# A scheduled RWKV and Fourier-mixing kernel: the first token DFT split in three, idle TensorE multiplications early, and a new order of all operations

## The chip, the cores and the metric

The kernel runs on one core of one Trainium2 chip. The metric is device time in microseconds (us), the median of the executions that are not disturbed. The kernel before took 244.32 and 245.5 us in its two undisturbed runs; a third, of 280.6 us, was slow (over 1.5% above the fastest of the same kernel), which is left out of comparisons.

TensorE (PE in the profile; its weight loads are PEld) multiplies, VectorE (DVE), ScalarE (ACT) and GpSimd (POOL) do the rest, SyncE (SP) issues most transfers (184 of 189 in the profile of before). One undisturbed execution of the same kernel differs from another by up to 1.4 per cent here, so differences of 1 us need many runs, and single profiles are compared only stretch by stretch.

## The reference

Four batches, eight heads, 768 tokens, head size 40. A recurrence over tokens, then a Fourier mixing with a small two-layer network on the 320 columns of all heads:

```python
for t in range(S):
    y[:, :, t] = einsum('bhd,bhde->bhe', r[t], state)
    Sa = einsum('bhde,bhe->bhd', state, a[t])
    state = state * w[t][:, :, None, :] - einsum('bhd,bhe->bhde', Sa, b[t]) \
            + einsum('bhd,bhe->bhde', v[t], k[t])
x = y.transpose(0, 2, 1, 3).reshape(B, S, 320)
u = x + real(fft(fft(x, axis=1), axis=2))        # token DFT, then column DFT
un = (u - mean(u)) / sqrt(var(u) + 1e-6)
out = u + relu(un @ w_ch1) @ w_ch2
```

## The kernel before

The kernel cuts the 768 tokens of a batch into six chunks of 128. Within a chunk the recurrence becomes matrix products. One function describes every operation once, with the engines that may run it; nothing is issued yet:

```python
# logarithm of the decay, split into a bf16 high part and a rest ("low")
op({"ACT": ... nc.scalar.activation(lg(), n_["w"](), Act.Ln)}, w=[logw], kind="ln")
op({"POOL": ..., "DVE": ... tensor_tensor(low, lg, hi, Alu.subtract)}, w=[low], r=[logw], kind="low")
# cumulated decays on TensorE, exponentials rw and wp on ScalarE, and the inputs scaled with them:
for j, nm, s_ in ((0, "k", rw), (2, "a", wp), (1, "b", rw)):
    op(scaled(nt[j], n_[nm], s_), kind="scale")               # VectorE or GpSimd, tile "nat"
# turned on TensorE, copied out of PSUM (kb, ar, vt), multiplied with each other,
op({"DVE": ... tensor_tensor(d_(), p2(), mask, Alu.mult),     # 128 x 1024 out of PSUM
    "ACT": ... activation(d_(), p2(), Act.Copy)}, kind="evac")
...
# the state
op({"DVE": ... tensor_tensor(s32(), Q(), wt(), Alu.mult)}, w=[s32], r=[Q, wt], kind="s32")
op({"ACT": ..., "DVE": ..., "POOL": ...copy(s16T, s32)}, w=[s16T], r=[s32], kind="s16T")
...
# tables of sines for the DFT: 15 small VectorE operations (tiles it, h), then ScalarE
# token DFT of a batch over its folded chunks (pm), in parts given by SPLIT
SPLIT = ((), (), (), (5,))
for c0, c1 in splits:
    for T in range(3): ... zmm(T, c0, c1)                     # kind "z"
```

Which engine runs what, in which order, and in which buffer, is written down in two strings, made by a search outside the kernel. `run` walks along them:

```python
def run(self, order, slots, warm):
    for i, e in order:
        if e == "WARM":
            warm(i // 64, i % 64)      # an idle multiplication into a free PSUM bank
            continue
        o = self.ops[i]
        before = set(o.preds) | self.take(o, slots)
        o.alts[e][1]()                 # issue it on engine e
        ...
```

Each engine works through its own operations strictly in that order: in the traces of before every engine's operations start in the order written (407 on VectorE, 3642 multiplications on TensorE).

## Time and profile before

| before | value |
|---|---|
| span of the profiled execution | 242.8 us |
| busy: TensorE, VectorE, ScalarE, GpSimd | 92%, 87%, 75%, 64% |
| VectorE's first eviction of a product (reading it out of PSUM, tile pr) | 16.52 us |
| VectorE's first addition of mixed values (hand-over) | 68.45 us |
| VectorE up to the hand-over: at work, idle | 61.81, 6.64 us |
| TensorE time lost after the hand-over | 13.5 us |

"Lost" is the distance between the starts of neighbouring TensorE instructions beyond their pace when dense, as the prediction defines it. Where TensorE is dense at full clock in the traces of before, the median distance is 25 ns for 40 columns, 56 for 128, 136 for 320 and 162 for 384, and of 64 rows and 128 columns two start every 55 to 56 ns. Turned means transposed.

### The profile page before, as it was taken

How to read it: one execution, taken by the hardware profiler on the slowest of the kernel's cores; microseconds unless marked ns; L12 is line 12 of the kernel's file. 1: busy time of each engine (PE TensorE's matmuls, PEld its weight loads, DVE VectorE, ACT ScalarE, POOL GpSimd, SP SyncE). 2: the span in 40 equal slices, each digit the busy share in tenths (PEclk: the TensorE clock that was granted, in tenths of full speed). 3: DMA queues.
4: the chain of work that ended last, by engine and by line, in shares of the span. 5: the costliest groups of instructions: out<-in, count | busy, mean ns of one | idle time of the engine just before them, and what ended most of it. 6: DMA issues, size and time to landing. Idle time of an engine off the chain costs nothing.

```text
span 242.8 us, 8954 instructions
## 1 busy us (share of the span) xinstructions
PE 223.3 (92%) x3642; PEld 172.9 (71%) x3642; DVE 210.2 (87%) x407; ACT 182.0 (75%) x379; POOL 156.5 (64%) x247
## 2 busy tenths in 40 slices
PE   0668979899999998999999999999999999999994
PEld 0436857778887776778887777788887778876672
DVE  6997999999899999979899998999999988488432
ACT  3595989898999987872799965974899988164620
POOL 7372594988896857845886878858996774510000
PEclk9995899999999999999999999999999999999999
DMA  7999999999773999999989999999899940011103
GB/s 121 187 184 157 189 163 159 160 158 162 122 128 52 180 170 133 166 162 185 162 160 244 182 166 178 162 167 150 214 175 165 146 47 4 3 54 63 47 27 135
DMA packets 171833, 33.94 MB, mean 140 GB/s; under 512 B 167120, under 2 KB 171472, under 8 KB 171792
## 3 DMA queue, kind: packets, MB, share of 16 engines
q1 hardware_dynamic: 170112, 31.73, 75.6%
q0 software_dynamic: 1680, 1.64, 4.8%
q8 instruction: 28, 0.46, 0.8%
q14 instruction: 13, 0.11, 0.1%
HBM read 26.87 MB, written 3.93 MB: 127 GB/s over the span
## 4 chain that ended last, share of the span: by engine, by line
PE 63%; DVE 18%; ACT 7%; issue 4%; SPq 3%; DMA 1%; POOL 1%; DVEq 0%; POOLq 0%
PE ps L152 63%; DVE h L152 4%; DVE pr L152 3%; DVE m L152 2%; SPq L416 2%; DMA in<-in_v_dram 1%; ACT pr L152 1%; DVE s L152 1%; SPq L752 1%; DVE xb L152 1%; DVE ps L152 1%; DVE ar L152 1%; DVE nat L152 1%; DVE xs L152 1%; ACT un L152 1%
## 5 line engine op out<-in xcount | busy, mean ns | idle before, releaser
L152 PE MATMUL ps<-unT,w1sb 128*128 128x384 bf16 x240 | 47.4, 326 | 0.4 <-ACT m L152 0.3
L454 POOL TENSOR_TENSOR nat<-in,rw 128x320 bf16<-128x320 f32 x41 | 35.7, 877 | 9.6 <-ACT rw L152 4.0
L152 DVE TENSOR_TENSOR pr<-ps,su 128x1024 bf16<-128x1024 f32 x31 | 37.4, 1216 | 1.4 <-PE ps L152 0.6
L152 PEld LDWEIGHTS <-nat 128*128 128x128 bf16 x512 | 31.4, 101 | 8.6 <-DVE nat L152 3.5
L152 ACT ACTIVATE pr<-ps 128x1024 bf16<-128x1024 f32 x33 | 33.4, 1028 | 3.8 <-PE ps L152 3.7
L152 PE MATMUL ps<-w2sb,h 128*128 128x320 bf16 x240 | 35.2, 299 | 0.0
L152 PEld LDWEIGHTS <-pr 128*128 128x128 bf16 x768 | 29.2, 96 | 6.8 <-issue 0.9
L152 PE MATMUL ps<-ident,nat 128*128 128x128 bf16 x352 | 31.6, 228 | 2.5 <-DVE nat L152 2.5
L447 POOL TENSOR_SCALAR_AFFINE_SELECT pr<-pr 128x1024 bf16<-128x1024 bf16 x28 | 30.6, 1096 | 4.9 <-ACT pr L152 4.7
L152 ACT ACTIVATE h<-ps 128x384 bf16<-128x384 f32 x56 | 26.5, 498 | 5.9 <-PE ps L152 5.6
L152 PEld LDWEIGHTS <-h 128*128 128x128 bf16 x240 | 22.7, 98 | 8.6
L152 PEld LDWEIGHTS <-w1sb 128*128 128x128 bf16 x240 | 20.6, 97 | 10.9 <-issue 0.6
L647 POOL TENSOR_TENSOR pm<-xb 128x161 bf16<-128x161 f32 x42 | 21.6, 530 | 7.0 <-DVE xb L152 6.9
L467 POOL TENSOR_TENSOR low<-logw 128x320 f16<-128x320 f32 x22 | 16.1, 736 | 13.8 <-issue 6.5
L454 POOL TENSOR_TENSOR nat<-in,wp 128x320 bf16<-128x320 f32 x20 | 17.6, 880 | 8.7 <-ACT wp L152 8.5
L152 PE MATMUL ps<-ar,kb 64*128 64x128 bf16 x384 | 18.1, 221 | 2.5 <-DVE kb L152 0.7
L152 DVE TENSOR_TENSOR m<-ps,su 128x1024 bf16<-128x1024 f32 x15 | 18.2, 1218 | 1.5 <-PE ps L152 1.4
L152 DVE SCALAR_TENSOR_TENSOR xb<-ps,bst,xb 128x320 f32<-128x320 f32 x24 | 12.8, 543 | 7.5 <-PE ps L152 5.8
L152 PE MATMUL ps<-nat,pr 128*128 128x40 bf16 x384 | 17.3, 180 | 0.5 <-DVE pr L152 0.4
L152 PE MATMUL ps<-xs,pr 128*128 128x40 bf16 x384 | 17.4, 181 | 0.2
L152 PEld LDWEIGHTS <-kb 64*128 64x128 bf16 x384 | 11.9, 95 | 7.1 <-issue 2.2
L152 ACT ACTIVATE sn<-ps 128x320 bf16<-128x320 f32 x22 | 9.8, 444 | 8.5 <-PE ps L152 7.9
(144 smaller groups left out, 573.8 us busy)
## 6 DMA issues: line engine op xcount, KB each, us to landing
in<-in_w_dram SPq DMA_DIRECT2D x24, 160.0 KB, 4.1
in<-in_v_dram SPq DMA_DIRECT2D x24, 160.0 KB, 3.7
in<-in_r_dram SPq DMA_DIRECT2D x24, 160.0 KB, 3.9
in<-in_a_dram SPq DMA_DIRECT2D x24, 160.0 KB, 3.9
in<-in_k_dram SPq DMA_DIRECT2D x24, 160.0 KB, 4.1
in<-in_b_dram SPq DMA_DIRECT2D x24, 160.0 KB, 3.9
out_dram<-xb SPq DMA_DIRECT2D x24, 160.0 KB, 2.3
w2sb<-in_moe_w_ch_dram POOLq DMA_DIRECT2D x2, 400.0 KB, 8.6
```

The source lines that it names most:

```text
L152: i = f(*args, **kwargs)
L416: op({"SP": (0.7, lambda x_=x_, t_=t_: nc.sync.dma_start(x_(), t_[bb, :, c * C:(c + 1) * C, :].rearrange("h t d -> t h d")))}, w=[x_], dma ...
L447: op({"POOL": (0.035 + 0.563 * n_, lambda d_=d_: nc.gpsimd.affine_select(out=d_(), in_=d_(), compare_op=Alu.is_gt, fill=0.0, base=0, patte ...
L454: return {"POOL": (0.82, lambda: nc.gpsimd.tensor_tensor(dst(), x_(), s_(), Alu.mult)), "DVE": (cD(320), lambda: nc.vector.tensor_tensor(d ...
L467: op({"POOL": (0.68, lambda: nc.gpsimd.tensor_tensor(low()[:, :, :D], lg(), hi()[:, :, :D], Alu.subtract)), "DVE": (cD(320), lambda: nc.ve ...
L647: op({"POOL": (0.46, lambda a_=a_, f_=f_: nc.gpsimd.tensor_tensor(*a_(), f_)), "DVE": (0.33, lambda a_=a_, f_=f_: nc.vector.tensor_tensor( ...
L752: op({"SP": (0.42, lambda c=c: nc.sync.dma_start(out[bb, c * C:(c + 1) * C], xb()[:, c, :DM]))}, r=[xb[c]], dma=0.5, kind="out")
```

## The change

The intent: keep TensorE's clock up early with idle multiplications (that they do so was my assumption), do the first batch's token DFT in parts as its chunks end, take PSUM banks beside held ones, drop a copy of the state, and search a new order under these rules. The diff, cut to its core (the strings are 46 and 11 lines long and change almost wholly; the rest is code for options that are switched off, and costs that only the search uses):

```diff
-ORDER = ("HWDAQDAUDAEDAHDAVDAIDAMGACGAAGAbSADGARDA+SBEAAfSCEGCFGCJDCIDCRDCGDABGAPDCLDBhSCHDAgSAXDASDAhAATGAiD"
...
+ORDER = ("AIDASDAJDAHDACGAFDARDA+SBEAABGCEGADGAbSAUDAQDAhABhSAgSAEDBFDAAGCFGA-WA-WA-WA-WA-WA-WAvWBJPBKAATDCHD"
...
-SPLIT = ((), (), (), (5,))
+SPLIT = ((3,5),(),(),(5,))
...
-            op({"DVE": ... nc.vector.tensor_tensor(s32(), Q(), wt()..., Alu.mult)}, w=[s32], r=[Q, wt], kind="s32")
-            op({... copy(d_(), s32())}, w=[s16T], r=[s32], kind="s16T")
+            if c == NCH - 2:
+                s32 = None
+                op({"DVE": ... nc.vector.tensor_tensor(d_(), Q(), decay(), Alu.mult)}, w=[s16T], r=[Q, wt], kind="s32")
+            else:
+                ... as before
```

A triple in ORDER is an operation and its engine; W stands for an idle multiplication. Which PSUM bank an operation takes is written in SLOTS alone.

## The prediction

> **What bounds the kernel now.** I began with the page's busy shares and its forty slices, to see whether one engine bounds the whole span. Its columns are tenths of busy time, one digit for 6.07 us.
>
> ```profile
> span 242.8 us, 8954 instructions
> PE 223.3 (92%) x3642; PEld 172.9 (71%) x3642; DVE 210.2 (87%) x407; ACT 182.0 (75%) x379; POOL 156.5 (64%) x247
> PE   0668979899999998999999999999999999999994
> DVE  6997999999899999979899998999999988488432
> PEclk9995899999999999999999999999999999999999
> ```
>
> The reader is to see two regimes. In the first eleven slices (67 us) VectorE is nearly always at 9 while TensorE has holes; after that TensorE is solid at 9. Only slices 4 and 5 have a reduced TensorE clock.
>
> TensorE's 92% overstates its load, because overlapping matmuls are counted to their modelled ends. So I summed what its instructions need at the pace of the dense stretches (columns / 2.4 GHz + 2.5 ns, never under 25 ns, half of that for the paired 64-row ones): 197.9 us, the six idle multiplications included. From its first matmul (5.59 us) to its last (239.2) pass 233.6 us, so 35.6 us are lost to waits and slow clock. By stretch: up to 68.4 us 22, from 68.4 to 239.6 us 13.5 (170.6 us for 157.1 us of work, 8%). Before the first matmul lie 5.6 us, after the last one 3.7.
>
> Next I took the stretches around the slow clock, and the chain of waits there.
>
> ```profile
> core 0: us, PE busy (x) PEld busy (x) DVE busy (x) ACT busy (x) POOL busy (x), PEclk, DMA share, GB/s
> 18.00:27.00 9.00, 8.19 (x119) 6.59 (x114) 7.21 (x12) 6.16 (x13) 2.15 (x4) 0.62 1.05 167
> 27.00:68.40 41.40, 38.22 (x816) 32.04 (x815) 38.84 (x59) 38.27 (x81) 35.15 (x53) 1.00 0.95 159
> 68.40:239.60 171.20, 169.03 (x2643) 129.38 (x2639) 147.59 (x302) 126.36 (x267) 107.76 (x151) 1.00 0.75 131
> ```
>
> ```profile
> 17.65 1.22 DVE pr L152
> 18.87 0.05 issue
> 18.91 2.82 PE ps L152 x39
> 21.75 0.70 DVE ar L152
> 22.50 9.26 PE ps L152 x161
> ```
>
> From 18 to 27 us TensorE is on the chain and VectorE has 1.8 us idle. From 27 to 68 us VectorE is busy 38.84 of 41.4 us: that stretch is VectorE's. From 68 us on TensorE alone is full (169.0 of 171.2).
>
> Last I took single instructions, for the clock itself and for the first batch's token DFT (columns: start, duration, engine; in brackets the idle time before it and who ended it):
>
> ```profile
> 19.37 0.43 PE L152 MATMUL ps<-logw,ut 128*128 128x320 bf16 x1
> 19.59 0.47 PE L152 MATMUL ps<-low,ut 128*128 128x320 f16 x1
> 19.85 0.63 PE L152 MATMUL ps<-ident,nat 128*128 128x128 bf16 x4
> ...
> 28.41 0.30 PE L152 MATMUL ps<-logw,ut 128*128 128x320 bf16 x1
> 28.55 0.30 PE L152 MATMUL ps<-low,ut 128*128 128x320 f16 x1
> ...
> 65.97 1.22 DVE L152 TENSOR_TENSOR m<-ps,su 128x1024 bf16<-128x1024 f32 x1 [0.85 <-PE ps L152]
> 68.45 0.49 DVE L152 TENSOR_TENSOR xb<-ps,xb 128x320 f32<-128x320 f32 x1
> ```
>
> The same 320-column matmul is followed after 0.26 us at 19.59 and after 0.14 us at 28.41: half the clock and the full clock. At 65.97 VectorE waits 0.85 us for a product that stands behind the token DFT (three groups of 12 column blocks, about 1 us each) in TensorE's order. The last line is VectorE's first addition of the mixed values (call it the hand-over): from there post-processing of batch 0 overlaps batch 1's chunks.
>
> [...] its clock records change at 12.36, 19.19 and 26.01 us, two gaps of 6.83 us[...]. [...]
>
> **The change, part by part.** I counted the operations of both programs and their order on each engine.
>
> 1. Clock. Idle multiplications go from 6 (2,712 columns) to 28 (11,760), nine of them before the first real matmul and 24 before batch 0's second chunk is far along. They use no other engine. In the slow stretch from 19.2 to 26.0 us TensorE did work worth 3.25 us at full pace in 6.9 us. If the clock holds, at most 3.6 us of that come back. But VectorE had only 1.8 us idle between 18 and 27, and it sets the rest: I count 1.5 us. The slow stretch before 12.4 us costs little, since the chain there runs over VectorE's tables.
>
> 2. VectorE's work before the hand-over. With the mean of each kind from the trace of before, its list up to there sums to 61.1 us before and 59.95 after: fewer wide evictions (24 to 22, 1.15 us each), scalings (6 to 3, 0.49) and zero fills (11 to 9), one select and one fold less, against 8 more small copies of turned tiles (0.43 each) and two more low parts (0.37). That is 1.1 us saved on the engine that bounds this stretch. Against it, fewer fills leave VectorE idle before the first logarithm (finished at 5.17 us): about 2.3 us idle at the start, where before had 1.7. Net 0.5 us.
>
> 3. Token DFT in three parts. The same matmuls, split 3 + 2 + 1 chunks. In the new order all nine groups still stand after the last chunk's output matmuls, within 14 TensorE operations, so they are not moved into early gaps. What is gained is that only 3 groups of 0.17 us wait for the last fold, and other work goes between: the 0.85 us wait at most; I count 0.5. The three banks are held only briefly.
>
> 4. State copy. In the last but one chunk of each batch the decayed state is written in bf16 directly: four copies fewer (0.4 us on ScalarE, 0.87 on VectorE), about 0.4 us off each batch's recurrence, which bounds nothing: 0.
>
> 5. The rest of the order. Counts for TensorE are the same, and at the first mixing matmul both kernels have the same 157.8 us of real TensorE work ahead. The gain of the first regime therefore goes through undiminished, and the second changes only by its 13.5 us of losses. A new order with retuned costs might take a tenth off these, but also lose it: I count 0.6 us of gain, give or take 2.
>
> Sum: 1.5 + 0.5 + 0.5 + 0.6 = 3.1 us. The two undisturbed runs of before, 244.32 and 245.5, average 244.9, so I predict 241.8 us, a ratio of 0.987. The hand-over should move from 68.45 to about 66 us.
>
> **Rivals.** (a) The clock's gain is wholly hidden: VectorE is busy at 9 through the first 67 us, so a faster TensorE only waits more. It speaks for this that slices 3 to 11 are VectorE's, against it that VectorE idled 1.51 us at 23.95 for TensorE. The time would be 243.5 to 245. (b) Idle multiplications get in the way: at half the clock their 10,400 early columns take 8.7 us in place of 4.4, in an in-order queue. A group of five (2,496 columns) stands before the third product of chunk 0; cold it takes 2.1 us. VectorE has three 1.2 us evictions to do meanwhile, so I expect at most 1 us. The time would be 245 to 247. (c) The order pays in the second regime: taking a third of its 13.5 us away would give 238. Nothing in the trace shows a large single wait to remove there (its longest named TensorE waits are under 0.5 us), so I hold it unlikely.
>
> **Range and chances.** Independent errors of about 1 us (clock), 1 us (VectorE's start) and 2 us (losses of the second regime) combine to 2.4 us, which with 8 in 10 gives 3.1: 238.8 to 244.9. Two per cent faster means under 240.0, which is 0.75 of such an error below the centre: 0.22. Two per cent slower means over 249.8: 0.03. Within: 0.75.
>
> **What would show it.** Right: a granted clock of 1.0 from about 12 us on, the 320-column pair near 20 us 0.14 us apart, the hand-over at 65 to 67 us, no 0.85 us wait before it, and 170 to 171 us of TensorE after it. Clock right but nothing gained (a): a hand-over after 67.5 us with VectorE busy throughout. (b) would show as first evictions later than 16.5 us. The prediction is wrong if the stretch after the hand-over changes by more than 3 us, or if the hand-over comes before 64 us, which VectorE's 59.95 us of work hardly allow.

## More of the kernel before

An operation that has to wait holds up everything behind it on its engine: in before, SyncE waits 13.2 us for the input of one transposing transfer, issues it at 75.08 us, and the loads behind it from 77.23 us on.

"At work" counts an operation to its end or to the start of the next; VectorE's very first fill, 0.27 us in every kernel, is counted as idle.

The prediction shows the page and the windows from 18 us on. It has nothing of the first 18 us but the clock, which turned out to be its gap. This is VectorE's timeline there (start, duration, engine, line, operation, output<-input, shapes):

```profile
7.50 0.43 DVE L152 TENSOR_TENSOR low<-logw 128x320 f16<-128x320 f32 x1
...
10.23 0.99 DVE L152 TENSOR_SCALAR h<-h 128x320 f32<-128x320 f32 x1
11.15 2.08 DVE L152 SCALAR_TENSOR_TENSOR h<-h,h 128x320 f32<-128x320 f32 x2
13.15 0.48 DVE L152 TENSOR_TENSOR nat<-in,wp 128x320 bf16<-128x320 f32 x1
...
15.14 1.33 DVE L152 TENSOR_SCALAR nsu<-su 128x128 bf16<-128x128 bf16 x1
15.91 0.68 DVE L152 COPY kb<-ps 128x1024 bf16<-128x1024 bf16 x1
16.52 1.21 DVE L152 TENSOR_TENSOR pr<-ps,su 128x1024 bf16<-128x1024 f32 x1
```

Two things are to be seen. The low part and the scaled input (nat<-in,wp), which TensorE waits for, stand behind small operations on the sine tables (h), which nobody needs before about 60 us. And some of these small operations are far longer than they need: 0.99 us for one on 320 columns, of which others take 0.32 us here, 2.08 us for the next two, and 1.33 us for the negation of a 128x128 mask.

## The result, and the profile after

The changed kernel took 237.97 us (four runs, 237.01 to 239.15); the kernel before, beside it, 244.58 in its three undisturbed runs (245.04 with the slow one). The ratio is 0.972, with an interval of 0.966 to 0.979: faster by 2.8%. A ratio is the mean time of one kernel's fast runs over that of the other's in the same rounds, so not quite the ratio of the medians. I timed the changed kernel twice more: 239.66 against 244.75 (0.980, 0.974 to 0.986) and 237.55 against 243.26 (0.976, 0.971 to 0.980), medians of fast runs. So the gain is 2 to 2.8%, about 5 to 7 us. I had predicted 3.1 us and held 238.8 as the lowest likely time; the prediction was wrong.

The page after (busy time; the forty slices):

```profile
span 235.7 us, 8993 instructions
...
PE 224.1 (95%) x3664; PEld 170.7 (72%) x3664; DVE 208.0 (88%) x411; ACT 182.3 (77%) x378; POOL 153.5 (65%) x242
...
PE   7878999889999999999999999999999999999994
...
DVE  6999999999999998998999999999899998689342
...
PEclk9999999999999999999999999999999999999999
```

TensorE begins in the first slice, with idle multiplications, and its granted clock has no hole from the first clock record (5.79 us) on. Before its first record the page prints full clock, but that isn't what ran: up to then idle multiplications of 504 columns start 0.42 us apart, half the pace of those at 9.05 us and later (0.21 us). The same goes for the kernel before up to 12.36 us (320-column matmuls 0.26 us apart at 8.51 us), whatever the rows for 0 to 18 us below say. The same stretches as in the prediction, with the first 18 us added (columns as there: PE, PEld, DVE, ACT, POOL busy, clock, DMA), first after, then the one line of before that was not shown:

```profile
0.00:18.00 18.00, 14.14 (x151) 7.62 (x152) 15.66 (x38) 12.40 (x26) 9.16 (x38) 1.00 0.97 160
18.00:27.00 9.00, 8.00 (x162) 5.91 (x159) 8.74 (x17) 8.97 (x17) 7.08 (x14) 1.00 1.00 171
27.00:63.40 36.40, 34.33 (x732) 28.60 (x728) 34.73 (x54) 32.58 (x71) 33.71 (x50) 1.00 0.95 161
63.40:232.50 169.10, 167.66 (x2631) 128.59 (x2628) 148.47 (x306) 128.33 (x269) 103.54 (x143) 1.00 0.80 138
```

```profile
0.00:18.00 18.00, 7.86 (x81) 4.86 (x81) 16.04 (x36) 11.21 (x21) 11.49 (x40) 1.00 1.02 164
```

The stretch between 27 us and the hand-over shrank from 41.4 to 36.4 us, the one after it from 171.2 to 169.1. GpSimd works 9.16 us in the first 18 in place of 11.49. From 18 to 27 us VectorE is now full, with 17 operations where it had 12.

The chain of waits after, where before had TensorE for 9.26 us from 22.50 on (start, duration, what; the longest pieces):

```profile
2.69 4.00 DMA in<-in_r_dram
...
10.82 1.01 ACT kb L160
...
13.40 1.22 DVE pr L160
...
17.70 2.32 ACT tk L160 x2
```

Its longest piece up to 26.7 us is now an input transfer, of 4.00 us: the start waits for data where it waited for tables. After that come pieces of ScalarE and VectorE: a copy on ScalarE, the first eviction, the sines. TensorE at half the clock is gone from it.

Clock and hand-over after (rows of TensorE, then of VectorE):

```profile
20.27 0.30 PE L160 MATMUL ps<-logw,ut 128*128 128x320 bf16 x1
20.41 0.30 PE L160 MATMUL ps<-low,ut 128*128 128x320 f16 x1
```

```profile
58.66 1.23 DVE L160 TENSOR_TENSOR m<-ps,su 128x1024 bf16<-128x1024 f32 x1
...
63.36 0.49 DVE L160 TENSOR_TENSOR xb<-ps,xb 128x320 f32<-128x320 f32 x1
```

The pair of 320-column matmuls is 0.14 us apart at 20 us, the last masked product before the hand-over no longer waits, and the hand-over comes at 63.36 us, 5.1 us earlier. Of these 5.1 us, VectorE's work makes 3.25 (61.81 to 58.56) and its idle time 1.84 (6.64 to 4.80). The work repeats in the two other profiles of the changed kernel (58.64 and 58.53), the idle time does not (5.99 and 4.83).

VectorE's start after, to be held against the block above:

```profile
2.85 0.13 DVE L160 TENSOR_SCALAR nsu<-su 128x128 bf16<-128x128 bf16 x1
...
5.64 0.49 DVE L160 TENSOR_TENSOR low<-logw 128x320 f16<-128x320 f32 x1
...
8.27 0.49 DVE L160 TENSOR_TENSOR nat<-in,wp 128x320 bf16<-128x320 f32 x1
...
13.40 1.21 DVE L160 TENSOR_TENSOR pr<-ps,su 128x1024 bf16<-128x1024 f32 x1
```

The mask takes 0.13 us at 2.85 us instead of 1.33 us at 15.14. The low part comes 1.9 us earlier and the scaled input 4.9 us earlier, with 14 and 8 of the 15 table operations still to come; the three copies of turned tiles are gone to ScalarE. The first eviction starts at 13.40 instead of 16.52 us (12.73 and 12.41 in the two other profiles).

The stretched operations of before have GpSimd at work beside them: GpSimd of before runs operations from 10.16 us to beyond 16.5 with at most 0.17 us between them, which is where 0.99, 2.08 and 1.33 us stand; after, it waits 6.82 us for an input, until 12.09. The first of them, in before:

```profile
10.16 0.88 POOL L454 TENSOR_TENSOR nat<-in,rw 128x320 bf16<-128x320 f32 x1 [3.84 <-ACT nat L152]
```

Over all operations of VectorE before the hand-over that took over 0.2 us more than the fast quarter of the same operation and shape, the excess is 3.5 us in the profile of before, and 1.2, 0.9 and 0.7 us in three profiles of the changed kernel. That GpSimd's work is the cause is read from this coincidence; no experiment of mine switched it alone, and how it would act is not shown. All twenty profiles together make the coincidence hard to escape: of 607 VectorE operations that worked on SBUF alone (statistics and fills left out) while GpSimd did nothing, none was stretched by over 0.2 us; of 458 with GpSimd busy for half their time or more, 191 were; of 5,763 that read or wrote PSUM, none was, whatever GpSimd did. So in these profiles GpSimd beside it is needed for a stretch, but is not enough. Counted in this way over all profiles, the stretching before the hand-over is 2.9 to 4.1 us in the seven that begin in the old order, and 0 to 1.5 us in twelve that begin in the new one; after_old_list has 2.6.

### The profile page after: what moved, and what is told of

It reads as the page before. It is cut to its first block, busy times and chain, and to the rows that moved or that the text cites.

```text
span 235.7 us, 8993 instructions
## 1 busy us (share of the span) xinstructions
PE 224.1 (95%) x3664; PEld 170.7 (72%) x3664; DVE 208.0 (88%) x411; ACT 182.3 (77%) x378; POOL 153.5 (65%) x242
## 4 chain that ended last, share of the span: by engine, by line
PE 52%; DVE 16%; ACT 12%; issue 6%; DMA 5%; POOL 4%; SPq 3%; DVEq 0%; POOLq 0%; ACTq 0%
PE ps L160 52%; DVE pr L160 4%; SPq L433 3%; DVE xb L160 2%; POOL nat L472 2%; DMA in<-in_k_dram 2%; DMA in<-in_r_dram 2%; DVE xs L160 1%; DMA in<-in_w_dram 1%; DVE sm L160 1%; ACT kb L160 1%; DVE h L160 1%; ACT L160 1%; ACT tk L160 1%; DVE un L160 1%
## 5 line engine op out<-in xcount | busy, mean ns | idle before, releaser
L160 PE MATMUL ps<-unT,w1sb 128*128 128x384 bf16 x240 | 45.9, 326 | 0.4 <-DVE xb L160 0.4
L465 POOL TENSOR_SCALAR_AFFINE_SELECT pr<-pr 128x1024 bf16<-128x1024 bf16 x31 | 34.4, 1116 | 8.9 <-ACT pr L160 8.7
L160 DVE TENSOR_TENSOR pr<-ps,su 128x1024 bf16<-128x1024 f32 x28 | 33.9, 1217 | 3.0 <-PE ps L160 2.6
L160 PEld LDWEIGHTS <-nat 128*128 128x128 bf16 x512 | 29.8, 97 | 7.6 <-DVE nat L160 1.5
L160 PE MATMUL ps<-ident,nat 128*128 128x128 bf16 x352 | 30.5, 219 | 1.2 <-DVE pr L160 0.3
L685 POOL TENSOR_TENSOR pm<-xb 128x161 bf16<-128x161 f32 x40 | 19.9, 523 | 2.8 <-DVE xb L160 2.8
L472 POOL TENSOR_TENSOR nat<-in,wp 128x320 bf16<-128x320 f32 x18 | 15.9, 881 | 8.5 <-PE ps L160 4.0
L160 DVE TENSOR_SCALAR h<-ps 128x384 bf16<-128x384 f32 x24 | 12.8, 551 | 3.4 <-PE ps L160 1.8
L488 POOL TENSOR_TENSOR low<-logw 128x320 f16<-128x320 f32 x17 | 12.2, 719 | 4.9 <-ACT logw L160 3.3
L160 DVE TENSOR_TENSOR m<-ps,su 128x1024 bf16<-128x1024 f32 x12 | 14.6, 1219 | 0.6 <-PE ps L160 0.5
```

Of the source, the lines that this page charges most:

```text
L160: i = f(*args, **kwargs)
L465: op({"POOL": (0.12 + 0.48 * n_, lambda d_=d_: nc.gpsimd.affine_select(out=d_(), in_=d_(), compare_op=Alu.is_gt, fill=0.0, base=0, pattern ...
L472: return {"POOL": (0.82, lambda: nc.gpsimd.tensor_tensor(dst(), x_(), s_(), Alu.mult)), "DVE": (cD(320), lambda: nc.vector.tensor_tensor(d ...
L488: op({"POOL": (0.68, lambda: nc.gpsimd.tensor_tensor(low()[:, :, :D], lg(), hi()[:, :, :D], Alu.subtract)), "DVE": (cD(320), lambda: nc.ve ...
L685: op({"POOL": (0.48, lambda a_=a_, f_=f_: nc.gpsimd.tensor_tensor(*a_(), f_)), "DVE": (0.33, lambda a_=a_, f_=f_: nc.vector.tensor_tensor( ...
```

## The experiments

Eighteen runs were made, of fifteen other kernels and three repeats; all gave correct results. They are told by the question they were to answer. Edits are written with names of operations in place of the codes of ORDER. "Ahead at W" is how much earlier than in the kernel before TensorE has done W us of useful work (idle multiplications not counted, each instruction at its dense pace). A caution first: with almost the same start, before_idle, before_direct_state and before_early_low have their hand-over at 67.39, 67.39 and 67.19 us, against 68.45 in the profile of before. About 1 us of its lateness is therefore the luck of that one execution, and of the 5.1 us a fairer figure is 4. The two other profiles of the changed kernel have theirs at 64.63 and 63.36, so single hand-overs differ by 1.3 us with nothing changed. Times and ranges in the table are over all runs; ratios use fast runs alone. Five rows hold slow runs: the medians of their fast runs are 237.71 (after_no_idle), 240.75 (after_no_idle_again), 239.46 (after_one_dft), 238.53 (after_late_low, two runs left) and 242.73 (before_direct_state).

| kernel | time (range, runs) us | ratio to before (95%) | hand-over us | VectorE work + idle up to it us |
|---|---|---|---|---|
| after_again | 239.66 (238.56–241.92, 6) | 0.980 (0.974–0.986) | 64.63 | 58.64 + 5.99 |
| after_third | 237.55 (236.75–238.83, 6) | 0.976 (0.971–0.980) | 63.36 | 58.53 + 4.83 |
| after_no_idle | 239.07 (237.03–241.78, 4) | 0.979 (0.972–0.987) | 63.22 | 58.88 + 4.35 |
| after_no_idle_again | 241.30 (239.03–243.99, 17) | 0.985 (0.981–0.988) | 63.08 | 58.38 + 4.70 |
| after_one_dft | 239.56 (237.89–244.1, 6) | 0.978 (0.972–0.985) | 64.81 | 58.42 + 6.39 |
| after_late_low | 241.14 (237.95–243.22, 4) | 0.975 (0.966–0.984) | 64.02 | 58.99 + 5.03 |
| after_old_list | 240.46 (239.36–242.35, 4) | 0.987 (0.981–0.993) | 65.95 | 61.22 + 4.73 |
| after_old_rest | 242.63 (241.56–243.83, 15) | 0.996 (0.994–0.999) | 63.74 | 57.80 + 5.94 |
| before_idle | 243.82 (242.63–245.39, 20) | 1.001 (0.999–1.003) | 67.39 | 61.79 + 5.60 |
| before_early_low | 243.68 (243.0–246.04, 20) | 1.000 (0.998–1.002) | 67.19 | 61.25 + 5.94 |
| before_direct_state | 242.75 (241.64–246.02, 20) | 0.996 (0.993–0.998) | 67.39 | 60.99 + 6.39 |
| before_all_parts | 246.66 (245.47–247.34, 6) | 1.013 (1.008–1.017) | 70.33 | 59.79 + 10.55 |
| before_front_new_rest | 246.43 (245.48–247.33, 4) | 1.012 (1.007–1.016) | 69.05 | 60.98 + 8.07 |

The kernels not in the table are told below with their times.

### Is it the clock?

after_no_idle and after_no_idle_again are the same kernel, the changed one without idle multiplications:

```diff
 ORDER of the changed kernel
-28 x W (idle multiplication)
```

> The kernel after with all 28 idle multiplications taken out, nothing else. Theory 1 (the clock carries the first stretch): [...] the hand-over (VectorE's first addition of mixed values, 63.36 us after, 68.45 before) comes at 66.5 us or later and the time rises by 3.5 us or more over the kernel after, to 241.5 us or more. Theory 2 (the new order of the first 20 us carries it, by relieving VectorE): the time rises by less than 1.5 us, to under 239.5 us. My prediction's own figure for the clock, 1.5 us, would give 239.5 us.

> The changed kernel without its 28 idle multiplications, timed more closely. Theory clock (the early full clock carries what my prediction gave it, 1.5 us or more): 1.5 us or more above after_again. Theory start-up list (what VectorE does first decides; the idle multiplications only steady the clock): within 1.0 us of after_again, with the wider spread from run to run.

> The changed kernel as it is, for a closer comparison with the two runs beside it. All theories: median between 237.0 and 239.2 us, ratio to the kernel before 0.970 to 0.980.

before_idle puts 18 idle multiplications early into the kernel before:

```diff
 ORDER of the kernel before
+8 x W before the first matmul, 10 x W between the first chunk's turns, products and its X
```

> The kernel before with 18 more idle multiplications of 504 columns in TensorE's early gaps (8 before the first real matmul, 10 between 12 and 19 us), order otherwise untouched. Theory 1 (clock): the clock is full from about 9 us on, the hand-over comes at 65.5 us or earlier, and the time falls by 3 us or more, to 242 us or less. Theory 2 (front order): VectorE's tables and fills still fill the first 16.5 us, so the time falls by 2 us at most, to 243 to 244.5 us, all of it from the stretch 18 to 27 us.

Without idle multiplications the clock was low until 9.40 us and again from 16.2 to 19.6 (in the repeat until 12.65 and from 16.1 to 19.5), and yet the hand-over came at 63.22 and 63.08 us, no later than with them. So no part of the early hand-over that these profiles can resolve is the clock's doing. With them in the kernel before, the clock was full from 11.8 us on, the hand-over 1.06 us earlier, as in other kernels without them, and the time the same (1.001). Where the whole time is concerned, the changed kernel was slower without them by 1.1 us in the medians of the fast runs of the same rounds and by 0.0044 in the ratios, which is 1.1 us of 245; the intervals overlap. So they may be worth about 1 us, not shown firmly, and not by way of the hand-over. I don't know the way.

The profile of after_no_idle_again shows what else can move single runs. It reached the hand-over first of all and then lost about 4 us against after_no_idle, between 63 and 80 us. These are the rows of GpSimd and VectorE there, then the same VectorE operation in after_no_idle with the GpSimd operation beside it:

```profile
74.74 0.44 POOL L531 CAST nat<-in 128x320 bf16<-128x320 f32 x1
75.15 0.85 POOL L471 TENSOR_TENSOR nat<-in,rw 128x320 bf16<-128x320 f32 x1
75.97 1.08 POOL L464 TENSOR_SCALAR_AFFINE_SELECT pr<-pr 128x1024 bf16<-128x1024 bf16 x1
```

```profile
75.62 3.18 DVE L159 TENSOR_SCALAR un<-xb,bst 128x320 bf16<-128x320 f32 x1
```

```profile
73.07 0.86 POOL L471 TENSOR_TENSOR nat<-in,rw 128x320 bf16<-128x320 f32 x1
73.65 0.47 DVE L159 TENSOR_SCALAR un<-xb,bst 128x320 bf16<-128x320 f32 x1
```

The same instruction took 0.47 us in one execution and 3.18 us in the other, in which GpSimd worked without a gap from 74.74 to about 79 us. In the first GpSimd was as busy (from 69.1 to 77.1 us), so a busy GpSimd alone doesn't decide; what does, these runs don't show. Before that, GpSimd had waited 2.17 us for an input transfer at 64.7 us, which it had not in the other. A late transfer shifts GpSimd against VectorE; that this shift made the collision is my reading of the two profiles, not shown by a run.

### Is it the DFT in three parts?

```diff
-SPLIT = ((3,5),(),(),(5,))
+SPLIT = ((),(),(),(5,))
 ORDER of the changed kernel
-z(chunks 0-2) x3, z(chunks 3-4) x3
```

> The changed kernel with the first batch's token DFT in one part again, its three groups of multiplications where the last part stood; all else as it is. Theory split (the prediction's third part, 0.5 us): 0.3 to 0.8 us above after_again. Rival: within 0.3 us, since in the order of the change all nine groups stand within 14 TensorE instructions of each other behind the last chunk, so that nothing is taken out of the hand-over by splitting.

It took 239.46 us in its fast runs, the changed kernel on the same chip 239.66. That fits the rival: the split is worth nothing that these runs resolve. But each ratio is known to about 0.006, or 1.5 us, so a gain of 0.5 us would not have been seen either. All nine groups stand within 14 TensorE instructions of each other behind the last chunk, with the split too.

### Is it VectorE's start?

after_late_low undoes one thing, before_early_low does some things alone:

```diff
 VectorE in the changed kernel (after_late_low)
-tab, low(chunk 0), 6 x tab, low(chunk 2)
+7 x tab, low(chunk 0), low(chunk 2)
```

```diff
 VectorE in the kernel before (before_early_low)
-fill(w1sb), zero fills, 6 x tab, low(chunk 0), 9 x tab, ... mask nsu between the copies
+zero fills, mask nsu, 3 x tab, low(chunk 0), 12 x tab, ... fill(w1sb) after the evictions
 SyncE
-load w(chunk 0), load w(chunk 1)
+load w(chunk 1), load w(chunk 0)
```

> The changed kernel with one thing of its start undone: on VectorE six small operations on tables stand again before the first low part (the remainder of the first chunk's logarithms), as in the kernel before. Theory start-up list (the gain of the first 15 us comes from the order in which VectorE does its first work, and is kept to the end): useful TensorE work of 2 us is reached 1.5 to 2.5 us later than in the changed kernel, VectorE's first addition of mixed values comes 1 us or more later, and the time is 240 us or more. Rival (the start has slack, VectorE's later work decides): the delay is gone by the first addition of mixed values, and the time is within 0.7 us of after_again.

> The kernel before with its start rearranged alone: the first two decay loads swapped, the first chunk's low part on VectorE behind three table operations instead of nine, the negated mask made at the head, the fill of the weights' tile made after the first evictions. Theory start-up order (it carries most of the earlier hand-over): useful TensorE work of 2 us is reached 1.5 us or more earlier than in the kernel before, and the first addition of mixed values comes 1 us or more earlier. Rival (the list of VectorE before the first eviction stays as long, only its order differs): the first eviction comes within 0.7 us of where it was, and the time is within 0.5%.

(In the kernel before the low part stands behind six table operations, not nine as I wrote.) Both runs go against the theory that the order of the start alone decides. Delaying the low part cost 0.9 us at the first eviction (13.40 to 14.31; 1.6 and 1.9 us against the two other profiles) and 0.9 to 1.3 us at W = 2, not 1.5 to 2.5, and of the four runs two were at 243.2 us, which count as slow, so the time settles nothing. Moving it forward in the kernel before (one zero fill of the low part on GpSimd goes forward with it) gained 0.3 us at the first eviction, and nothing in time. What came next on VectorE, the scaled input, still stood behind all tables.

after_old_list puts the length of the list back:

```diff
 ORDER of the changed kernel
-ACT: copy vt, copy ar, copy kb of chunk 0       (0.41 + 0.69 + 0.69 us on VectorE, without overlaps 1.53)
+DVE: copy vt, copy ar, copy kb of chunk 0
-DVE: mask nsu at the head, fill(w1sb) at 55 us
+DVE: fill(w1sb) at the head, mask nsu between the copies
```

> The changed kernel with VectorE's list before the first eviction as long as it was: the three turned copies back on VectorE, the fill of the weights' tile back at the head, the negated mask late; order otherwise as in the change. Theory list (step 2 of the prediction, with its sizes): first eviction 2.0 to 2.5 us later than in the changed kernel (0.59 us fill, 1.53 us copies, 0.13 us mask), first addition of mixed values 1.0 us or more later, ratio to the kernel before 0.980 to 0.986. Rival (absorbed in VectorE's later idle time): the delay is under 0.5 us by the first addition of mixed values.

The first eviction came 1.55 us later (14.95), the hand-over 2.59 us later (65.95), and the ratio was 0.987. VectorE's work up to the hand-over was 61.22 us, as much as in the kernel before, and its idle time as small as in the changed kernel. So the hand-over followed the work: this theory holds. Against the two other profiles of the changed kernel the delays are 2.2 and 2.5 us at the first eviction, as expected, and 1.3 and 2.6 at the hand-over. The edit itself adds only the copies, 1.53 us, to the work up to the hand-over (fill and mask stand before it in both orders); of the 2.66 us by which the work grew, about 1.4 is more stretching (2.6 us in place of 1.2). By the three ratios of the changed kernel (0.972, 0.980, 0.976) these few operations are worth 0.7 to 1.5% of the time, 1.6 to 3.6 us; against 0.980 alone, from the same chip, the intervals overlap.

before_all_parts puts everything that can be taken singly into the kernel before: the edits of before_early_low, the three copies on ScalarE, the 18 idle multiplications, and the direct state.

```diff
 ORDER of the kernel before
+the edits of before_early_low and before_idle
-DVE: copy vt, copy kb, copy ar of chunk 0
+ACT: copy vt, copy kb, copy ar of chunk 0
+state written directly in the last chunk but one
```

> The kernel before with all the parts that I could put in singly: the first loads swapped, low part early, mask early, fill late, the three turned copies of the first chunk on ScalarE, 18 idle multiplications early, the state written directly in the last chunk but one of each batch. The order is otherwise that of before. Theory parts (their gains add up: start and list about 2 us, direct state about 1 us, idle multiplications 0 to 1): ratio to the kernel before 0.984 to 0.989. Theory whole order (each is absorbed by the waits that the old order has at the hand-over): 0.993 or more.

> The changed kernel again, beside before_all_parts: ratio to the kernel before 0.970 to 0.981.

It was slower, by 1.3%, worse than both theories allow, while the changed kernel beside it had 0.976. VectorE's list was shorter by 2.0 us, but its idle time grew to 10.55 us. Its rows:

```profile
12.53 1.14 DVE L152 TENSOR_TENSOR nat<-in,wp 128x320 bf16<-128x320 f32 x1
...
15.73 2.48 DVE L152 TENSOR_TENSOR pr<-ps,su 128x1024 bf16<-128x1024 f32 x2 [1.66 <-PE ps L152]
```

The scaled input is still done only at 13.7 us, behind the tables. Only then can TensorE turn it and ScalarE copy it, at 1.01 and 1.02 us for a tile where VectorE takes 0.68, one after the other. VectorE waits 1.66 us for them. In the changed kernel the scaled input is ready at 8.8 us, so the copies can run on ScalarE while VectorE does the tables. The scaled input itself was stretched there, to 1.14 us. That the copies pay on ScalarE only when the tables stand behind the inputs is read from these rows; what before_all_parts shows is that the parts do not add.

before_new_front and before_new_front_idle give the kernel before the first 178 operations of the new order, without and with idle multiplications:

```diff
 ORDER of the kernel before
-operations up to the first chunk's dx
+the changed kernel's first operations, then what was left of the old ones in their old order
```

> The code of before with the first 178 operations in the order and on the engines of the kernel after, up to the second chunk's recurrence (about 23 us), but with no idle multiplications in it; the rest in the order of before. Theory 1 (clock): under 1.5 us gained, 243.5 us or more, with a reduced clock before 27 us. Theory 2 (front order): first eviction near 14 us in place of 16.5, 3 to 4.5 us gained, 240.5 to 242 us.

> The same with the idle multiplications of the kernel after in the front. Both theories: the second chunk's recurrence at 24 us as in the kernel after (29.1 before), 5 us gained if the rest of the order of before lets it pass, so 239.5 to 240.5 us; the remaining 2 us up to the kernel after are then the order of the rest. If much less than 5 us is gained, the old rest gives it back.

The first work came early: 4.66 us ahead at W = 2 without idle multiplications. By W = 18 it was 3.6 us behind, because the operations that the new order had put off (the fill, logarithms, copies) now stood in a heap at the seam. The clock was low there as well, for 20.5 us between 17 and 41 us, and with idle multiplications for 13.7 us between 17 and 45; whether as a cause or a consequence, these runs don't show. The times were 248.24 (ratio 1.021) and 249.01 us (1.023).

### Is it the order after the hand-over?

after_old_rest and before_front_new_rest exchange the halves:

```diff
 ORDER (after_old_rest)
 the changed kernel's up to the hand-over
-the changed kernel's after it
+that of the kernel before after it
```

```diff
 ORDER (before_front_new_rest; on the changed kernel's code, no idle multiplications)
-the changed kernel's up to the hand-over
+that of the kernel before up to the hand-over
 the changed kernel's after it
```

> The code of after, in its own order up to the hand-over (5.1 us earlier than before), and in the order of before from there on, the stalling transfer included. Theory 3: the stall comes back, the last input lands 2 us or more later than in the kernel after (188.0), and most of the front's gain is lost: 240.5 us or more. Rival (the front's gain of 5.1 us goes through, the rest of the order is worth the remaining 2 us): 239.5 to 240 us with the last input no later than 189.5.

> The counterpart of after_old_rest: the order of the kernel before up to the hand-over (no idle multiplications), the new order from there on, on the changed kernel's code. Theory rest alone (the new rest saves TensorE's waits after the hand-over whatever stood before): TensorE's lost time after the hand-over 11 to 12 us instead of 13.2, ratio to the kernel before 0.985 to 0.993. Rival (the two halves of an order fit each other; joined to another front, a rest loses at the seam): ratio 0.997 or more, as after_old_rest kept only 3 of 7 us.

after_old_rest was 5.5 us ahead at the hand-over (W = 40), lost 3.2 of them by W = 50, and ended 3.0 ahead in the profile, 0.4% in time. The loss sits at the seam: TensorE loses 1.58 us at 69.78, where VectorE frees a bank, and 0.68 at 71.19 (lost as defined above; the profile's own idle figures are about 0.16 us lower each). before_front_new_rest went from 1.2 us ahead at W = 26 to 2.6 us behind at W = 50, made up 2.1 us by the end, and was slower than the kernel before. Here the rival's numbers came in both: a rest fits the front that it was found with. What is lost at a seam cannot be booked to the rest or to the front, so I cannot say what the new rest is worth alone. The two figures there are, the 2.1 us by which the stretch after the hand-over shrank, and the 4.2 us by which the changed kernel beats after_old_rest in the profiles (7.2 against 3.0), measure different things.

### Is it the input stream, or the state?

The first transposing transfer of the second batch holds SyncE's queue for 13.2 us in the kernel before, so I suspected the loads behind it. Three kernels issue loads ahead of such transfers:

```diff
 SyncE
-dmaT (waits for its input), load, load, ...
+load, load, ..., dmaT
```

> The kernel before with one edit: in SyncE's in-order queue the 13 input loads that stood behind the first transposing transfer of batch 1 (which was ready at 75.05 us, while the slots of those loads were free from 53.8 us on) now stand ahead of it. Theory 3 (the input stream bounds the second regime; that stall cost it some 5 us): the DMA share between 70 and 80 us goes from 0.49 to 0.9 or more, the last input lands near 188 us in place of 193.4, and the time falls, by 3 us or more if nothing else bounds, by 0.5 to 2 us if TensorE's path from a hand-over at 68.45 us takes over at once. Rival (TensorE alone bounds the second regime, as I predicted): the stall was hidden, the time stays within 0.5 us.

> The same with six loads put ahead of the first transposing transfer of batch 1. Theory 3: last input 2 us or more earlier than in the run without it, and 1.5 us or more of time regained. Rival: no change beyond 0.5 us.

> The kernel after with up to four loads put ahead of each of the 16 transposing transfers where the order list has their slots free. If the input stream still bounds the kernel after, the last input lands before 187 us and the time falls by 1 us or more, to 237 us or less; if TensorE bounds it now, nothing changes; if the transfers now come too late for their products, it slows.

before_loads_past (13 loads) landed its 72nd load at 78.0 instead of 89.5 us, and took 246.79 us, ratio 1.010. after_old_rest_loads_past (6 loads) took 242.26, ratio 0.995, as without. after_loads_past, with up to 4 loads ahead of each of 16 transposes, took 247.88, ratio 1.016: its TensorE loses 6.02 us at 91.8 and 1.90 us at 83.8 for the transposes, which now come late. The theory of the input stream finds no support: none of the three gained time. As every one of them also put transposes back, the runs don't separate what earlier inputs alone would be worth; transposes that come late cost much.

```diff
-s32 = Q * wt ;  s16T = copy(s32)          # in the last chunk but one of each batch
+s16T = Q * wt
```

> The kernel before with the decayed state of each batch's last chunk but one written directly in bf16, four copies fewer. Theory of the prediction (nothing, as the copy stands on ScalarE or GpSimd off the path): within 0.3% of the kernel before. Rival (it shortens the chain from the state to the next chunk): 0.5% or more faster.

It took 242.75 us, ratio 0.996 with an interval of 0.993 to 0.998: between the two expectations, and not nothing. That is 1.1 us (0.6 to 1.6) of 244. In its profile 0.5 us come at W = 120 and 0.2 at W = 170, in the later batches.

## Why the prediction was wrong

The gain in the medians of fast runs was 244.58 - 237.97 = 6.6 us in the first comparison, 5.1 and 5.7 us in the two later ones, against a predicted 3.1. So the sum was about half of what came. By its steps:

1. **Clock, 1.5 us.** The record of the clock is as predicted, 0.14 us at 20 us included (one reading was off: seven, not nine, idle multiplications stand before the first real one). The gain is not at the hand-over, where the runs without idle multiplications are as early (63.22 and 63.08 us against 63.36). Up to about 1.1 us may come back in the whole time, which the runs do not resolve. The rival (a) that I had named describes the hand-over better: VectorE sets it, and a faster TensorE only waits.

2. **VectorE's list, net 0.5 us. This step failed.** "With the mean of each kind from the trace of before, its list up to there sums to 61.1 us before and 59.95 after." The count of operations was right and so was the idle start. But a mean duration is not a property of an operation. Operations that ran beside GpSimd were stretched, 3.5 us in all, and the new order took most of that away, which no count shows. The work fell by 3.25 us: 1.1 counted, and about 2.3 by which the stretching is less (3.5 to 1.2). I had written that 59.95 us of work hardly allow a hand-over before 64 us; the work was 58.56, and the hand-over at 63.36. The second half of the failure is the idle time, which I let grow and which fell by 1.84 us (by 0.65 and 1.81 in the two other profiles, so this half is less sure): the scaled input came out 4.9 us earlier, so TensorE and ScalarE had the first products ready when VectorE had finished the tables. I had taken the stretch before 18 us for harmless ("the chain there runs over VectorE's tables") and had not asked whether the tables must stand there. after_old_list shows that work put back on this list delays the hand-over, before_all_parts that cutting it in the old order does not pay.

3. **DFT in three parts, 0.5 us.** Not resolved: undone, the medians differ by 0.2 us the other way, with 1.5 us of uncertainty in each ratio. That all nine groups stay behind the last chunk was in the prediction; the 0.85 us wait did vanish from the trace.

4. **State copy, 0.** Measured 1.1 us (0.6 to 1.6) in the kernel before. "About 0.4 us off each batch's recurrence, which bounds nothing" was too quick.

5. **The rest of the order, 0.6 us, give or take 2.** The stretch from the hand-over to the end shrank by 2.1 us in the first profile, by 0.7 and 0.9 us in the two others. This lies inside what I allowed, but it adds up with step 2 instead of cancelling. In the first profile the 2.1 us come between W = 60 and W = 70 (1.8 us; 1.1 and 0.9 in the two other profiles), where the kernel before waits for products and banks: 0.43 us at 94.17, 0.59 at 95.11, 0.35 at 102.52. They are single losses of at most 0.6 us; I had said that there was no large one to remove, and did not ask for their sum. Rival (c), that the order pays after the hand-over, is right in part at most.

"The gain of the first regime therefore goes through undiminished" holds for the changed kernel, 5.1 us at the hand-over and 7.2 at the end (3.8 and 4.5, 5.1 and 5.9 in the two other profiles). It is no rule: after_old_rest kept 3.0 of 5.5 us, and before_idle 0.3 of 1.06.

Together, of the 7.2 us between the two profiles, 5.1 arise before the hand-over, 1 of it the bad luck of the profiled execution of before, and 2.1 after it. What stays open is how much of the rest's 0.7 to 2.1 us the direct state brings, and how the idle multiplications act, if they do.

## What to carry to other kernels

Before summing an engine's list with mean durations, look for single operations that take twice what others of their shape take, and ask what ran beside them. At the start of a kernel look for work that nobody waits for yet (here tables needed at 60 us) in front of the first inputs on the same in-order engine. And in a searched order don't expect parts to add: moved alone, the pieces of this 2 to 2.8% gain changed the time by anything from 0.4% faster to 2.3% slower.
